# Batch 0's query sketch with tokens as rows, one numerator path, W_out in 2 KB rows, and a new order of work

## The chip, the cores and the metric

The kernel runs on one core of one Trainium2 chip. The metric is the device time of one execution in microseconds; of several executions the median is given. The core has five instruction streams that run side by side and meet only at semaphores: TensorE (PE; its weight loads are shown apart as PEld), VectorE (DVE), ScalarE (ACT), GpSimd (POOL) and SyncE (SP). In this kernel SP only issues DMAs; ScalarE issues a few.

## What is computed

Attention with polynomial sketches in four batches of four heads, 1088 tokens and 32 dimensions, then a feed-forward stage with a tanh shrink over all 4352 tokens:

```python
def phi(x):                      # r = 8, so 64 features
    a = np.einsum('rd,bhsd->bhsr', S1, x)
    b = np.einsum('rd,bhsd->bhsr', S2, x)
    return np.einsum('bhsi,bhsj->bhsij', a, b).reshape(*x.shape[:-1], 64)
q_p, k_p = phi(q), phi(k)
kv  = np.einsum('bhsf,bhsd->bhfd', k_p, v)
z   = np.sum(k_p, axis=2)
num = np.einsum('bhsf,bhfd->bhsd', q_p, kv)
den = np.einsum('bhsf,bhf->bhs', q_p, z)[..., None] + 1e-06
x = (num / den).transpose(0, 2, 1, 3).reshape(4352, 128)
h = x @ w_in                     # 128 -> 2048
out = (h - np.tanh(h)) @ w_out   # 2048 -> 128
```

Inputs and output are fp32. The attention matmuls run in fp32, the feed-forward ones in bf16.

## The kernel before

**A planned order.** The program is a list of operations (`_Prog.add`) with the tiles that they read and write. `TABLE` is the order, written out: each token is an operation's number, the engine that runs it (`v`, `a`, `g`, `t`, `s` for VectorE, ScalarE, GpSimd, TensorE, SP) and the buffers that it takes; `f` and `F` are matmuls on zeros of 256 and 512 columns (L423, L424). `plan` walks through the table, gives out buffers and adds a dependence for each reuse of one; it also holds a big load back until all but 1.45 MB of the big loads ahead of it have landed. `sync` turns dependences into semaphore waits, and `emit` writes the five streams. Each engine runs its own operations strictly in the table's order. An operation can carry `lock=True`; before, nothing reads it.

**Attention of a batch.** k is transposed by VectorE in 32x32 blocks (L530), sketched by TensorE (L575), and transposed back into `abk` (L587). A gram matrix of the two k sketches (L602) is copied out (`gm`), multiplied by S2 (`scmm`, L612 or L614) and copied into the query's weights (`wqd` for batch 0, `wq` through `scx` and `sc`, L622 and L626, for the others): this gives the denominator as one more sketch column group. The 64 products of a token's two k sketches are formed in `w` (L642) by VectorE or GpSimd, and 36 matmuls (L657) multiply them by v. The result is copied four times over (`kvd`), transposed on TensorE (L675) and copied to `kvb`. q is transposed by VectorE (L567) and sketched by TensorE with the sketch weights stationary (L753, 32x32 tiles of the array); the result comes back to tokens as rows by a VectorE transpose into `abc` (L758). Then `m`, `den`, `rd`, `aq` (tile `ap`) form the first sketch divided by the denominator (L770 to L778); `qp` (L796) forms the products, `qpT` (L801) transposes them, `num` (L812) multiplies them by `kvb`, and two copies `x` put the tokens into `xT`, the feed-forward input, in bf16.

**Batch 0** has two parts. Its first 384 tokens take a path of their own, `q_heads` with `kv_heads` (L685 to L731): K·V in a block-diagonal form `kvd_68`, the sketch as one 128x128 matmul (L700), `abc` by a VectorE transpose (L703), and the numerator as four fp32 matmuls (L731). Its other 704 tokens take the common path.

**Weights.** W_in is loaded in four pieces of 512 columns and cast to bf16 (`wi`, L353); W_out likewise (`wo`), its loads in rows of 512 bytes: partition `ji` takes row `jb * 128 + ji`. W_in is also transposed on TensorE (L881, `wit`) and copied (`wiT`), and W_in times W_out is formed once (L895) and split into `wch` and `wcl`.

**Feed-forward.** The tokens go in ten groups (`GCOLS`: 384, 352, 352, six of 512, 192). A group has 16 matmuls `h` (L917) of up to 512 tokens, each into a PSUM bank out of three; ScalarE takes tanh of it (`th`, L921), which frees the bank; 16 matmuls `o` (L938) add up the output, and two matmuls (L942) with `wch` and `wcl` add the linear part. From the eighth group on two banks are taken at a time, and for part of the columns of groups 5 to 8 VectorE adds the linear part (L926). The group's result is transposed by VectorE (`ot`, L947) into one of three tiles and stored by four or eight DMAs (L957).

## Time and profile before

| | us |
|---|---|
| median of 3 runs | 104.42 (103.82 to 105.89) |
| the profiled execution | 105.08 |
| its span, first to last instruction | 102.8 |
| PE busy / DVE / ACT / POOL | 96.5 / 79.5 / 79.1 / 36.4 |
| first feed-forward matmul | 17.16 |
| batch 1's numerator | 40.28 |
| last transpose of the output | 99.43 |
| bytes moved | 11.37 MB |

A busy PE isn't PE at its peak: the end of a matmul is modelled, and zero matmuls count as busy. A row of the timeline gives the start, the busy time, the engine, the line, the operation, the tiles (written <- read), the shapes and the count; in brackets stands how long the engine was idle before it and what ended that. SPq and ACTq are DMA issues. fp32 matmuls appear as two passes, so a group of 36 has a count of 72. Numbers of lines are those of the kernel before.

### The profile page before, as it was taken

Reading aid. Unit: us, or ns where it says so; the run is one execution under the profiler, and the core shown is the slowest. Engines: PE = TensorE matmul, PEld = TensorE weight load, DVE = VectorE, ACT = ScalarE, POOL = GpSimd, SP = SyncE. Lnnn points to the kernel's source line nnn. Section 1 sums busy time; section 2 is a strip of 40 time slices with the busy share of each in tenths; the row PEclk is TensorE's granted clock in tenths of the full one; section 3 lists DMA queues with packets and bytes.
Section 4 is the critical chain, followed back from the end, with each engine's and each line's share of the span. In section 5 each row is a group of like instructions: output and inputs, shape, how many; then the busy total and the mean of one; then the engine's idle time right before and its main releaser. Section 6 shows DMA issues by size and latency. Waiting matters only on the chain.

```text
span 102.8 us, 3036 instructions
## 1 busy us (share of the span) xinstructions
PE 96.5 (94%) x1260; PEld 48.2 (47%) x1260; DVE 79.5 (77%) x145; ACT 79.1 (77%) x157; POOL 36.4 (35%) x54
## 2 busy tenths in 40 slices
PE   5999979999969999999999999999999999999960
PEld 2343556466625545453733444343454444445650
DVE  1669799759748999798579699678899789999530
ACT  4001298986559989799899698999996999999940
POOL 3079845740044594099994890000000000000000
PEclk9999999999999999999999999999999999999999
DMA  2887968979999670311300003304200320501555
GB/s 69 269 270 228 298 216 244 307 223 282 323 267 242 169 183 0 53 24 28 48 0 6 0 0 55 54 0 68 34 0 11 57 41 0 90 12 17 79 74 83
DMA packets 25917, 11.37 MB, mean 111 GB/s; under 512 B 19120, under 2 KB 23600, under 8 KB 25904
## 3 DMA queue, kind: packets, MB, share of 16 engines
q1 hardware_dynamic: 24288, 10.98, 42.2%
q10 hardware_dynamic: 1616, 0.20, 1.3%
q8 instruction: 10, 0.16, 0.7%
q14 instruction: 3, 0.02, 0.1%
HBM read 8.95 MB, written 2.23 MB: 109 GB/s over the span
## 4 chain that ended last, share of the span: by engine, by line
PE 68%; DMA 15%; SPq 10%; DVE 2%; issue 1%
PE psb L917 27%; PE psb L938 27%; SPq L459 10%; DMA wi_f<-in_moe_w_in_dram 6%; DMA wo_f<-in_moe_w_out_dram 5%; PE psb L812 4%; DMA qL<-in_q_dram 4%; PE psb L942 3%; PE psb L753 2%; PE psb L657 2%; DVE qT L567 1%; PE psb L575 1%; DVE abk L587 1%; PE psb L602 0%; PE psb L675 0%
## 5 line engine op out<-in xcount | busy, mean ns | idle before, releaser
L917 PE MATMUL psb<-xT,wi 128*128 128x512 bf16 (+3 forms) x160 | 48.8, 349 | 0.0
L921 ACT ACTIVATE th<-psb 128x512 bf16<-128x512 f32 (+3 forms) x77 | 40.5, 599 | 2.8 <-PE psb L917 2.4
L938 PE MATMUL psb<-th,wo 128*128 128x512 bf16 (+3 forms) x90 | 26.4, 343 | 0.1
L917 PEld LDWEIGHTS psb<-xT,wi 128*128 128x128 bf16 x160 | 14.7, 97 | 23.1 <-ACT th L921 4.1
L921 ACT ACTIVATE wi_f<-psb 128x512 bf16<-128x512 f32 (+3 forms) x31 | 16.6, 623 | 1.6 <-PE psb L917 1.5
L921 ACT ACTIVATE wo_f<-psb 128x512 bf16<-128x512 f32 (+2 forms) x28 | 16.7, 630 | 1.4 <-PE psb L917 1.3
L796 POOL TENSOR_TENSOR qp<-ap,abc 128x768 f32<-128x768 f32 x11 | 16.4, 1511 | 3.6 <-DVE ap L778 3.4
L926 DVE TENSOR_TENSOR th<-psb,th 128x320 bf16<-128x320 f32 (+2 forms) x24 | 13.4, 563 | 1.9 <-ACT th L921 1.0
L642 POOL TENSOR_TENSOR w<-abk 128x768 f32<-128x768 f32 x7 | 11.1, 1594 | 8.4 <-DVE abk L587 8.4
L938 PEld LDWEIGHTS psb<-th,wo 128*128 128x128 bf16 x90 | 8.8, 100 | 5.6 <-POOL wo L353 0.5
L938 PE MATMUL psb<-wo_f,wo 128*128 128x512 bf16 (+1 forms) x32 | 10.9, 363 | 0.0
L801 DVE STREAM_TRANSPOSE qpT<-qp 128x768 f32<-128x768 f32 x11 | 10.4, 956 | 0.5 <-POOL qp L796 0.5
L938 PE MATMUL psb<-wi_f,wo 128*128 128x512 bf16 (+2 forms) x38 | 10.3, 344 | 0.0
L947 DVE STREAM_TRANSPOSE ot<-psb 128x512 f32<-128x512 f32 (+3 forms) x10 | 6.3, 633 | 3.4 <-PE psb L938 3.3
L424 PE MATMUL psb<-zz 128*128 128x512 bf16 x24 | 8.1, 468 | 0.0
L926 DVE TENSOR_TENSOR wi_f<-psb,wi_f 128x192 bf16<-128x192 f32 (+1 forms) x12 | 6.1, 510 | 1.6 <-ACT wi_f L921 0.9
L926 DVE TENSOR_TENSOR wo_f<-psb,wo_f 128x320 bf16<-128x320 f32 (+2 forms) x12 | 6.8, 572 | 0.7 <-ACT wo_f L921 0.3
L530 DVE STREAM_TRANSPOSE kT<-kL 128x576 f32<-128x576 f32 (+3 forms) x10 | 5.8, 606 | 1.6 <-DMA kL<-in_k_dram 1.6
L758 DVE STREAM_TRANSPOSE abc<-psb 128x1152 f32<-128x1152 f32 (+1 forms) x4 | 5.1, 1272 | 1.9 <-PE psb L753 1.8
L812 PE MATMUL psb<-qpT,kvb 32*32 32x288 f32 (+1 forms) x256 | 6.2, 392 | 0.0
L567 DVE STREAM_TRANSPOSE qT<-qL 128x1088 f32<-128x1088 f32 (+2 forms) x5 | 5.2, 1057 | 0.6 <-DMA qL<-in_q_dram 0.6
L657 PE MATMUL psb<-w,vL 128*32 128x64 f32 x288 | 5.2, 221 | 0.0
(89 smaller groups left out, 98.1 us busy)
## 6 DMA issues: line engine op xcount, KB each, us to landing
vL<-in_v_dram SPq DMA_DIRECT2D x16, 144.0 KB, 3.8
kL<-in_k_dram SPq DMA_DIRECT2D x8, 272.0 KB, 3.3
qL<-in_q_dram SPq DMA_DIRECT2D x6, 272.0 KB, 4.2
wi_f<-in_moe_w_in_dram SPq DMA_DIRECT2D x4, 256.0 KB, 5.9
wo_f<-in_moe_w_out_dram SPq DMA_DIRECT2D x4, 256.0 KB, 5.6
out_dram<-ot SPq DMA_DIRECT2D x14, 64.0 KB, 2.0
out_dram<-ot SPq DMA_DIRECT2D x8, 48.0 KB, 3.1
qL<-in_q_dram SPq DMA_DIRECT2D x2, 176.0 KB, 3.4
```

Of the source, the lines that this page charges most:

```text
L424: "F": lambda e, n: e.matmul(bank(3), zz.ap[:, 0:128], zz.ap[:, None, 128:384].to_broadcast([128, 2, 256]), start=True, stop=True)}, zop)
L459: op = P.add({x: occ for x in (eng if isinstance(eng, tuple) else (eng,))}, lambda e, n: e.dma_start(out=o_, in_=i_), w=w, dma=(nbytes, nb ...
L642: P.add({**_v(768), **_gt(768)}, lambda e, n: e.tensor_tensor(out=wv.ap.rearrange("p (x i j) -> p x i j", i=8, j=8), in0=abh(0)[:, :, :, N ...
L657: i = e.matmul(pv[b].ap[h * 32:(h + 1) * 32, 0:64], vL[b][:, h, blk * 32:(blk + 1) * 32], wvs[b, p].ap[:, (bi * 4 + h) * 64:(bi * 4 + h + ...
L796: P.add({**_v(cn * 256), **_gt(cn * 256)}, lambda e, n, qp=qp, c0=c0, cn=cn: e.tensor_tensor(out=qp.ap[:, 0:cn * 256].rearrange("p (x i j) ...
L801: P.add(_v(cn * 256), lambda e, n, qp=qp, o0=o0, cn=cn: e.transpose(qt.ap[:, o0 * 256:(o0 + cn) * 256], qp.ap[:, 0:cn * 256]), r=[qp], w=[ ...
L812: i = e.matmul(psa4[h * 32:(h + 1) * 32, g, 0:nb * 32], kvb.ap[g * 32:(g + 1) * 32, x, h * 32:(h + 1) * 32], qq[g * 32:(g + 1) * 32, 0:nb, ...
L917: P.add(_mm(n_), lambda e, n, jb=jb, hv=hv: e.matmul(hv.ap[:, jb % m * 512:jb % m * 512 + n_], wi[jb // 4].ap[:, (jb % 4) * 128:(jb % 4 + ...
L921: act = P.add(_a(n_ * m), lambda e, n, hv=hv, th=th: e.activation(out=th.ap.rearrange("p (u x) -> p u x", u=m)[:, :, 0:n_], in_=hv.ap.rear ...
L926: P.add(_vp(gc * m), lambda e, n, hv=hv, th=th: e.tensor_tensor(out=th.ap.rearrange("p (u x) -> p u x", u=m)[:, :, 0:gc], in0=hv.ap.rearra ...
L938: fn = lambda e, n, x=x, st=st, sp_=sp_: e.matmul(ov.ap[:, 0:n_], wo[x // 4].ap[:, x % 4, :], ths[x][0].ap[:, ths[x][1] * 512:ths[x][1] * ...
L947: P.add(_vp(n_), lambda e, n: e.transpose(ot.ap[:, 0:n_], ov.ap[:, 0:n_]), r=[ov], w=[ot], name=f"ot{gi}")
```

## The change

- **Batch 0's query sketch.** `q_heads` and `kv_heads` are gone. All of batch 0's q is sketched by nine matmuls (three operations of three, `q_sketch0`) in which q's transpose is the stationary side and the weights `wqd`, now 24 columns a head, are the moving one. The result has tokens as rows, and three plain copies on ScalarE bring it into `abc`, in place of VectorE's transposes. The zero columns of `wqd` and their memset go, as does `sc` of batch 0.
- **One numerator path.** The first 384 tokens of batch 0 take the common path, `q_front` and `q_piece`, with `kvd`, its transpose and `kvb` ahead of it.
- **W_out in 2 KB rows.** Partition `ji` of piece `i` takes the four rows `i * 512 + ji * 4` to `+ 3`, 2 KB in one run. So that W_in's columns agree, its cast reads every fourth column.
- **Turns.** A `lock` operation on VectorE waits for the last `lock` operation before it on GpSimd, and the other way round.
- **Loads.** Three of batch 0's v loads and one of W_in are issued by ScalarE, and v waits until the second half of k has landed.
- **New order.** All of `TABLE` is new. By the engines' streams: the program opens with twelve long zero matmuls; ScalarE's queue is `abc0.0`, `abc0.6`, a W_in cast, `kvd0`, a W_in cast, `abc0.3`, `kvb0`, `wiT0` and the copy of the first tokens; ScalarE also casts a third W_in piece and two W_out pieces, GpSimd the rest; the W_in cast `wi2` stands ahead of the first tanh; W_out's loads stand ahead of batch 1's v and batch 2's k; of the three k products of a batch, batch 0 has two on VectorE (before: one) and batch 1 none (before: all three); VectorE takes the q transposes of batches 1 and 2 ahead of `abc` of batch 1; `gm` of batches 2 and 3 go to VectorE, `kvb` of 2 and 3 to ScalarE; output stores are issued later and in another order.

```diff
--- before.py
+++ after.py
@@ TABLE @@
...
@@ plan @@
+        lastl = {"vector": None, "gpsimd": None}
...
+            if o.lock and e in lastl:
+                d = lastl["gpsimd" if e == "vector" else "vector"]
+                if d is not None:
+                    o.deps.setdefault(d, False)
+                lastl[e] = o
@@ tiles @@
-    qpTh_p = pool("qpTh", 2, [128, 6 * 64])
-    wqd = sb("wqd", [128, H, 32])
+    wqd = sb("wqd", [128, H, 24])
-    kvd0 = sbv("kvd0", [128, 2, 128])
-    P.add(_g(32), lambda e, n: e.memset(wqd[:, :, 24:32], 0.0), w=[wqdc], name="wqdz")
@@ loads @@
-                load_s(1, S2, ("scalar", "sync"))
+                load_s(1, S2, "sync")
...
-            load(vL[b][:, h, :], src, [vvals[b][h]], 128 * 1152, 128, ("sync", "scalar") if b == 0 else "sync", name=f"lv{b}.{h}", occ=640.0)
+            load(vL[b][:, h, :], src, [vvals[b][h]], 128 * 1152, 128, ("sync", "scalar") if b == 0 else "sync", name=f"lv{b}.{h}", occ=640.0, wait=[x for x in P.ops if x.name == "lk0.1"] if b == 0 else ())
...
-    wos = moe_w_out.rearrange("(jb ji) c -> ji jb c", jb=NJB, ji=128)
+    wos = moe_w_out.rearrange("(i ji jb) c -> ji i (jb c)", i=4, jb=4)
...
-        load(wof[i].ap, wos[:, i * 4:(i + 1) * 4, :], [wof[i]], 128 * 2048, 512, name=f"lwo{i}")
+        load(wof[i].ap.rearrange("p j c -> p (j c)"), wos[:, i, :], [wof[i]], 128 * 2048, 128, name=f"lwo{i}")
@@ batch 0's q @@
-    def kv_heads():
...
-    def q_heads(i):
...
+    def q_sketch0(s0, s1, abc):
+        outs = []
+        for j, a in enumerate(range(s0, s1, 3)):
+            pq = _Val(first1)
+
+            def sk(e, n, a=a, pq=pq):
+                for k in range(3):
+                    i = e.matmul(pq.ap[:, k * 96:(k + 1) * 96], qTs[0][:, (a + k) * 128:(a + k + 1) * 128], wqd.rearrange("p h f -> p (h f)"),
+                                 start=True, stop=True, skip_group_check=True)
+                return i
+            P.add(_pe(550, 230.0), sk, r=q_in(0, a, a + 3) + [wqds, wqdc], w=[pq], mode="128x128", name=f"qsk0.{a}")
+            outs.append((j, a, pq))
+        for j, a, pq in outs:
+            P.add({**_a(288), **_vp(288)}, lambda e, n, a=a, pq=pq: copy(
+                e, n, abc.ap[:, a - s0:a - s0 + 3, :, 0:24], pq.ap[:, 0:288].rearrange("p (k h f) -> p k h f", h=H, f=24)),
+                r=[pq], w=[abc], name=f"abc0.{a}")
...
-            cn = 2 if left in (2, 4) else min(left, 3)
+            cn = 2 if left in (2, 4) or (b, s0) == (0, 0) else min(left, 3)
+            cn = min(cn, left)
...
-        q_sketch(b, s0, s1, abc)
+        q_sketch0(s0, s1, abc) if b == 0 else q_sketch(b, s0, s1, abc)
...
-        kv_heads()
-        q_heads(0)
+        kv_tail(0)
+        q_transpose(0, 0)
+        st = q_front(0, 0, 3)
+        q_piece(0, 0, 0, 3, *st)
@@ weights @@
-            P.add({**_as(512), **_g(512), **_v(512)}, lambda e, n, i=i: copy(e, n, wi[i].ap[:, :], wif[i].ap), r=[wif[i]], w=[wi[i]], name=f"wi{i}", lock=True)
+            P.add({**_as(512), **_g(512), **_v(512)}, lambda e, n, i=i: copy(
+                e, n, wi[i].ap.rearrange("p (b j) -> p b j", b=4), wif[i].ap.rearrange("p (j b) -> p b j", b=4)), r=[wif[i]], w=[wi[i]], name=f"wi{i}", lock=True)
```

More of the change, by code (lines that the diff above doesn't have):

```diff
@@ L70 @@
+821v:1 823s 824a 825a 822s
 """
@@ L544, in s_weights @@
         for i, (w, z) in enumerate(zip(wqc, wqs)):
+            if i == 0:
+                continue
             P.add(_g(8), lambda e, n, z=z: e.memset(z[:, 24:32], 0.0), w=[w], name=f"wqz{i}")
@@ L631, in gram @@
                 e, n, wqds.ap, pg.ap[:, 64:96].rearrange("p (h i) -> p h i", h=H)), r=[pg], w=[wqds], name="wqs0")
-            P.add(_v(32), lambda e, n: e.tensor_reduce(
-                out=wqs[b][:, 16:24], in_=wqds.ap.rearrange("p h i -> p i h"), op=ALU.add, axis=AX.X),
-                r=[wqds], w=[scv[b]], name=f"sc{b}")
     wvs = {}
@@ L680, in kv_tail @@
             r=[pv[b]], w=[kvb], name=f"kvb{b}")
-    kvh = _Val(ap=sb("kvh", [128, 64]))
-    def kv_heads():
-        P.add(_vp(64), lambda e, n: e.transpose(kvh.ap, pv[0].ap[:, 0:64]), r=[pv[0]], w=[kvh], name="kvh")
-        P.add({**_v(256), **_gt(256)}, lambda e, n: e.tensor_tensor(
-            out=kvd0.ap.rearrange("p x (h v) -> p x h v", h=H),
-            in0=kvh.ap.rearrange("p (x v) -> p x v", x=2)[:, :, None, :].to_broadcast([128, 2, H, 32]),
-            in1=maskh.ap[:, None, :, None].to_broadcast([128, 2, H, 32]), op=ALU.mult),
-            r=[kvh, maskh], w=[kvd0], name="kve", lock=True)
@@ L853, in attention @@
         q_transpose(0, 1)
-        kv_tail(0)
         st = q_front(0, 3, 9)
```

128 lines of the change are left out of this document (42 added, 86 removed).

## The prediction

> **What bounds the kernel now.** I read the page's busy times, then busy time by stretch, then the chain that ended last. Stretches show PE, PEld, DVE, ACT and POOL busy with counts, the granted clock, the DMA share and GB/s.
>
> ```profile
> PE 96.5 (94%) x1260; PEld 48.2 (47%) x1260; DVE 79.5 (77%) x145; ACT 79.1 (77%) x157; POOL 36.4 (35%) x54
> ...
> 0.00:17.16 17.16, 15.17 (x222) 7.70 (x223) 12.56 (x31) 6.45 (x12) 9.61 (x28) 1.00 0.74 226
> 17.16:40.28 23.12, 22.20 (x384) 11.73 (x390) 18.43 (x30) 18.67 (x51) 11.04 (x12) 1.00 0.81 232
> 40.28:99.43 59.15, 59.11 (x667) 28.82 (x666) 48.13 (x85) 53.99 (x95) 15.73 (x14) 1.00 0.20 31
> ```
> ```profile
> 7.15 5.79 DMA wi_f<-in_moe_w_in_dram
> ...
> 23.04 4.41 DMA qL<-in_q_dram
> 27.47 1.31 DVE qT L567
> 28.78 0.74 DVE abk L587 x2
> 29.66 1.04 PE psb L753 x32
> ...
> 40.28 1.53 PE psb L812 x63
> ...
> 51.04 0.22 PE psb L675 x2
> ...
> 99.43 0.38 DVE ot L947
> ```
>
> There are three stretches. Until 17.16 batch 0's attention runs, and much of TensorE's work is the zero matmuls of L424. From 17.16 to 40.28 FFN and attention of batches 1 and 2 share TensorE; the chain goes through loads until batch 1's q (27.47), its sketch (29.66) and its numerator (40.28). After 40.28 TensorE is full for 59.1 of 59.15 us. ScalarE idles 4.45 us in the second stretch and 5.2 in the third. So three things can move the end: the start of the FFN, batch 1's numerator, and ScalarE, once it has less slack than it is given work. The last transpose starts at 99.43 of a 102.8 span; that tail keeps its four stores on SP and ACT.
>
> **The start, step by step.** These rows carry it.
>
> ```profile
> 1.31 4.08 PE L424 MATMUL psb<-zz 128*128 128x512 bf16 x10
> 6.42 0.81 PE L424 MATMUL psb<-zz 128*128 128x512 bf16 x3
> 6.50 2.02 SPq L459 DMA_DIRECT2D wi_f<-in_moe_w_in_dram  x4
> 7.31 0.34 PE L602 MATMUL psb<-abk 128*32 128x32 f32 x17
> 7.33 1.51 POOL L642 TENSOR_TENSOR w<-abk 128x768 f32<-128x768 f32 x1 [0.49 <-DVE abk L587]
> 8.38 0.18 ACT L353 COPY wqd<-psb 128x32 f32<-128x32 f32 x1 [0.43 <-PE psb L614]
> 8.43 1.23 DVE L642 TENSOR_TENSOR w<-abk 128x768 f32<-128x768 f32 x1
> 9.03 0.30 PEld L700 LDWEIGHTS psb<-qT,wqd 128*128 128x128 f32 x2 [0.46 <-POOL wqd L442]
> 10.41 1.23 PE L657 MATMUL psb<-w,vL 128*32 128x64 f32 x72
> 11.57 1.04 PE L424 MATMUL psb<-zz 128*128 128x512 bf16 x4
> 12.31 0.62 ACT L353 CAST wi<-wi_f 128x512 bf16<-128x512 f32 x1 [3.75 <-DMA wi_f<-in_moe_w_in_dram]
> 12.84 0.36 ACT L353 COPY kvd<-psb 128x256 f32<-128x256 f32 x1
> 13.25 0.44 PE L675 MATMUL psb<-ident,kvd 128*128 128x128 f32 x2 [0.64 <-ACT kvd L353]
> 15.13 1.52 PE L731 MATMUL psb<-qpTh,kvd 128*128 128x192 f32 x8
> 16.56 0.55 ACT L353 CAST xT<-psb 128x192 bf16<-128x192 f32 x2
> 17.16 0.66 PE L917 MATMUL psb<-xT,wi 128*128 128x384 bf16 x3
> ...
> 23.60 1.35 PE L812 MATMUL psb<-qpT,kvb 32*32 32x192 f32 x64
> ```
>
> Zero matmuls: twelve long ones open the program instead of ten and a short one (4.08/10 = 0.41 each), and five and a half instead of three and a half (0.81/3 = 0.27 each) stand ahead of the gram. I let the gram start at 7.8, not 7.31.
>
> Query sketch: before, TensorE waited 0.46 for POOL's memset of `wqd`; that goes. From the gram to the end of the `wqd` copy is 8.56 - 7.31 = 1.25, so the sketch starts at 9.1, as now. Now it ends at 10.41, 1.4 later. The new one is nine fp32 matmuls, each recorded as two passes, of 96 columns with q's transpose as weights. A pass costs 0.22/2 = 0.11 in the transpose of `kvd` (128 columns) and 1.52/8 = 0.19 at L731 (192 columns). So 18 passes cost 2.0 to 3.4. I take 2.0, because 96 columns is nearest the first row; with its zero matmuls it ends at 11.2.
>
> K·V: 1.23 as now, to 12.4. Then `kvd`. Now it stands in ScalarE's queue behind a w_in cast that waits for its load until 12.31, though K·V was done at 11.64. In the new order w_in's first load is the eighth issue on SP (three v loads go to ScalarE's queue), about 4.6 by the present issues; with the 5.8 us it takes now it lands near 10.4, and the cast is over when K·V ends. So `kvd` runs 12.45 to 12.8. If that cover fails, `kvd` is late by as much as the load is. Behind the v loads, which wait for K, stand only the table load and the gram's copy at about 8.
>
> TensorE meanwhile has four zero matmuls (1.04) and one set of W_in transposes (0.25 estimated from 0.22 to 0.44 for two wider ones), so the `kvd` transpose runs 13.7 to 14.1 and `kvb`, now on ScalarE, 14.1 to 14.5. The numerator has 64 passes of 96 columns: under the 1.35 of the 192-column one and, at worst, no cheaper than it. I take 1.1, ending at 15.6, result at 15.85. The copies out run side by side on VectorE and ScalarE (0.55/2 each), so the FFN starts near 16.3, **0.9 earlier**.
>
> VectorE's path to that numerator: two k products behind POOL's turn (7.6 + 1.51 = 9.1, then 0.9 each from the row of three below), four small steps of about 0.25, two products and two transposes of 0.6: 13.5. It has 1 us of cover. The turn by semaphore itself costs no work here: VectorE's product already took 1.23 instead of 0.9 when it began while POOL's ran (8.43 against 8.84).
>
> The bounds of the start are -1.5 (zero matmuls hidden, numerator at 1.0) and +0.6 (sketch at 3.4, less cover).
>
> The Trainium skill speaks against one edit. Its page "SBUF — State Buffer", section "Door 1: The DMA port swizzle", says that SBUF works in 16-byte lines and that each access in a new line pays a penalty. W_out in 2 KB rows makes the W_in casts read every fourth fp32, one per line. No row here shows such a read.
>
> I keep the casts at 0.62, the row of the same size. The nearest row of a read with gaps is POOL's `m` below, eight of every 32 fp32: 0.79/288 = 2.7 ns an element, against 1.51/768 = 2.0 in a product, 1.4 times. The upper end is twice 0.62, an estimate: each element a second access. Three of the four casts are on ScalarE: one ahead of `kvb` (+0.6 at that end) and one ahead of the first tanh (+0.6).
>
> **The middle.**
>
> ```profile
> 8.93 2.10 POOL L642 TENSOR_TENSOR w<-abk 128x768 f32<-128x768 f32 x1
> ...
> 22.14 2.69 DVE L642 TENSOR_TENSOR w<-abk 128x768 f32<-128x768 f32 x3
> ...
> 24.99 0.42 ACT L353 CAST xT<-psb 128x320 bf16<-128x320 f32 x1 [0.79 <-PE psb L812]
> ...
> 28.23 0.37 ACT L353 COPY kvb<-psb 128x256 f32<-128x256 f32 x1
> ...
> 30.80 1.38 DVE L758 STREAM_TRANSPOSE abc<-psb 128x1152 f32<-128x1152 f32 x1 [1.29 <-PE psb L753]
> ...
> 32.26 0.79 POOL L770 TENSOR_TENSOR m<-abc 128x288 f32<-128x288 f32 x1 [1.16 <-DVE abc L758]
> ...
> 33.13 0.21 ACT L353 COPY gm<-psb 128x32 f32<-128x32 f32 x1
> ...
> 34.56 4.45 POOL L796 TENSOR_TENSOR qp<-ap,abc 128x768 f32<-128x768 f32 x3 [1.51 <-DVE ap L778]
> ```
>
> The first copied tokens (batch 0's second part) follow the start. In the new order its numerator stands behind `scx`, and `scx` behind POOL's first k product of batch 1; queued behind `scx` on VectorE are batch 2's k transposes. From 14.0 POOL has five short steps of about 0.6 (a W cast's time) and three products of 1.51: 21.5. TensorE comes to the numerator 23.60 - 17.16 = 6.4 after the start, as now: 22.7. So the turn has 1 us of cover; without it batch 2's transposes and this numerator are late by the rest of a product, up to 1.5.
>
> Batch 1: equal bytes precede its q on the queues in both orders. W_out's four loads are ahead of it, in 2 KB instead of 512 B pieces, and SP no longer stops for W_in so late. If the rate is unchanged (226, then 232 GB/s), q arrives as now. The DMA engines idle 0.26 of 17.16 us and 0.19 of the next ten, 6.4 us; if a fifth of it goes, q is 1.3 earlier. VectorE takes both batches' q transposes (1.31 each) ahead of `abc`, and batch 2's q comes 0.56 MB later, 2.4 us. So `abc` ends near 31.0 instead of 32.18, or, with the rate unchanged, as now. From there to the numerator it is 40.28 - 32.18 = 8.1 now: 2.4 until POOL's first product, 4.45 for three, the rest for transposes. In the new order it is 2.4, a product on VectorE (0.9), `scx` (0.2), two on POOL (3.0), a transpose (0.9) and up to 0.7 for an output transpose in between: 8.1 again.
>
> ScalarE gets ahead of that numerator two W_out casts (0.62, as W_in's), a copy of 0.5 (0.42 at five sixths of its size) and loses the gram copy (0.21) and two tanh (0.4 each), +0.7, and one W_in cast (0.62) before its first tanh. With the present idle of 4.45 the start's gain would be gone; without the wait for batch 1's q it is at 38.9. I take the numerator at 39.1, **1.2 earlier, start included**; bounds -2.2 and +0.2.
>
> **The rest.** TensorE's work is the same to 0.2. ScalarE takes two `kvb` (0.37 each), a larger x copy and one tanh or two from before, less a gram copy: +1.3 into 5.2 us of idle. Nothing to all of it may come back; I take +0.5, nearer to nothing, because TensorE is the full one (59.11 of 59.15). Output stores stand in a new order on SP; a transpose that reuses a tile waits for its old stores. They are issued a group or more ahead in the order, which hides them; without that cover one transpose is late by a landing:
>
> ```profile
> out_dram<-ot SPq DMA_DIRECT2D x14, 64.0 KB, 2.0
> ```
>
> **Sum.** -1.2 + 0.5 = -0.7. The profiled execution took 105.08, 2.28 beyond its span and 0.66 above the median, so it would be 104.4; against the median of 104.42 the forecast is **103.7**. From no change a measurement of this kernel can tell about 2%.
>
> **Rivals.** *The start carries through.* The start is at its lower bound (-1.5), the 0.92 that TensorE is seen idle in the second stretch (23.12 - 22.20) goes with the earlier q, and ScalarE's additions vanish in its idle time: -2.4, 102.0. The load at 27.47 speaks for it, the equal 8.1 us behind it against it.
>
> *ScalarE becomes the bound.* It has 18.67 + 53.99 = 72.7 busy us behind the start and gets 2.7 more (three casts 1.86, copies 1.24, less 0.42), one cast of it ahead of the first tanh. If its idle comes from dependences and stays, the first tanh is 0.75 earlier and the last 2.1 - 0.75 = 1.4 later: 105.8. With the strided casts at twice their time, 1.2 more: 107.0, slower. It decides from +2.1, that is, once a strided cast takes 0.97 and the idle stays. The 5.2 us of idle in the full stretch speak against it; that each FFN matmul needs a bank that a tanh frees speaks for it.
>
> *The change doesn't do what it says:* the turns take nothing away, since the two engines already exclude each other at 8.43, and W_out's rows matter only if the load rate bounds. Then only the new order counts, at 104.4.
>
> **How the numbers follow.** Forecast 0.50, of it the case of 104.4 0.15; the start carries through 0.18; ScalarE the bound 0.32, 0.24 of it with the casts' price and beyond 106.5. Range 101.7 to 107.0, which takes in both rivals' times and leaves less than 2 in 10 outside; the likeliest case alone spans 102.5 to 104.9. Faster by over 2% (under 102.3) 0.18, within 2% 0.58, slower (over 106.5) 0.24.
>
> **What would show it.** First FFN matmul near 16.3; the sketch's passes near 0.11; W_in casts at 0.62, or near 1.2 if the lines count; the numerator of batch 1 at 39.1; ScalarE's idle after it under 4 us; no wait over 0.5 between VectorE and POOL that TensorE then waits for. Wrong if the W_in loads land after 12, if a turn holds VectorE ahead of a transpose that TensorE needs, or if tanh comes late in the third stretch.

## The result and the profile after

The changed kernel is slower by 0.7%: 105.24 us median (104.08 to 107.57, 20 runs) against 104.44 (103.48 to 105.89, 20 runs) of the kernel before, ratio 1.0066 with a 95% interval of 1.0040 to 1.0093. The forecast was 103.7. The loss is smaller than the 2% by which one measurement can tell a change, but its interval lies clear of 1. All ratios here take only each kernel's undisturbed runs within 1.5% of its fastest, so they can differ from the quotient of two medians, most where a kernel's times spread widely.

The busy times of the page after, and busy time by the same three stretches (until the first FFN matmul, until batch 1's numerator, until the last output transpose; columns as in the prediction):

```profile
PE 96.5 (93%) x1305; PEld 50.0 (48%) x1305; DVE 77.9 (75%) x140; ACT 82.0 (79%) x161; POOL 35.9 (35%) x50
```
```profile
0.00:16.89 16.89, 15.43 (x264) 8.96 (x265) 10.77 (x26) 7.02 (x13) 7.10 (x28) 1.00 0.75 234
16.89:40.55 23.66, 21.82 (x389) 12.03 (x394) 18.17 (x30) 19.83 (x52) 15.40 (x14) 1.00 0.69 211
40.55:99.81 59.26, 59.22 (x667) 28.97 (x667) 48.55 (x86) 55.15 (x98) 13.42 (x10) 1.00 0.22 35
```

TensorE's work is the same to the tenth (96.5 each). The stretches took 16.89, 23.66 and 59.26 us where they took 17.16, 23.12 and 59.15: the start gained 0.27, the middle lost 0.54, the full stretch lost 0.11. Behind the last transpose's start stand 3.59 us (103.4 - 99.81) instead of 3.37. Together that is +0.60, the difference of the spans (103.4 to 102.8). TensorE idled 1.84 us in the middle stretch (23.66 - 21.82), twice the 0.92 of before. So the start gained too little, and something new stands in the middle.

The chain that ended last, after (start, length, what), names both; its first three rows are the new sketch:

```profile
9.50 0.68 PE psb L691 x6
10.28 0.64 PE psb L691 x6
11.04 0.66 PE psb L691 x6
12.12 1.06 ACT wi L359
13.45 1.03 ACT wi L359
...
16.50 1.04 ACT wi L359
...
25.73 0.91 PE psb L659 x54
26.64 1.58 issue
28.22 0.49 PE psb L659 x18
...
40.55 1.53 PE psb L775 x63
```

Before, no cast of W_in was on this chain. Now three are, of over 1 us each. And inside batch 1's K·V (L659) stands 1.58 us of "issue", time in which TensorE waits for nothing that the profile shows. In the order of time, the start of the same trace:

```profile
12.01 1.17 ACT L359 CAST wi<-wi_f 128x512 bf16<-128x512 f32 x1
13.08 0.37 ACT L359 COPY kvd<-psb 128x256 f32<-128x256 f32 x1
13.34 1.14 ACT L359 CAST wi<-wi_f 128x512 bf16<-128x512 f32 x1
...
14.67 0.38 ACT L359 COPY kvb<-psb 128x256 f32<-128x256 f32 x1
...
16.40 1.14 ACT L359 CAST wi<-wi_f 128x512 bf16<-128x512 f32 x1
17.42 0.51 ACT L886 ACTIVATE th<-psb 128x384 bf16<-128x384 f32 x1
```
```profile
7.96 0.34 PE L607 MATMUL psb<-abk 128*32 128x32 f32 x17
...
9.34 0.84 PE L691 MATMUL psb<-wqd,qT 128*128 128x96 f32 x6
...
11.72 1.21 PE L659 MATMUL psb<-w,vL 128*32 128x64 f32 x72
...
15.20 0.95 PE L775 MATMUL psb<-qpT,kvb 32*32 32x96 f32 x64 [0.16 <-ACT kvb L359]
...
16.89 0.49 PE L882 MATMUL psb<-xT,wi 128*128 128x384 bf16 x2
```

A W_in cast takes 1.14 to 1.17 us instead of 0.62. One stands ahead of `kvd`, one ahead of `kvb`, one ahead of the first tanh. The middle, from a timeline of all engines:

```profile
25.66 0.98 PE L659 MATMUL psb<-w,vL 128*32 128x64 f32 x54
...
26.70 1.29 DVE L572 STREAM_TRANSPOSE qT<-qL 128x1088 f32<-128x1088 f32 x1
...
28.22 0.49 PE L659 MATMUL psb<-w,vL 128*32 128x64 f32 x18 [1.58 <-issue]
...
28.75 0.37 ACT L359 COPY kvd<-psb 128x256 f32<-128x256 f32 x1 [2.37 <-PE psb L659]
...
29.05 1.31 DVE L572 STREAM_TRANSPOSE qT<-qL 128x1088 f32<-128x1088 f32 x1 [1.05 <-DMA qL<-in_q_dram]
...
31.23 1.38 DVE L720 STREAM_TRANSPOSE abc<-psb 128x1152 f32<-128x1152 f32 x1 [0.87 <-PE psb L715]
```

Each fp32 matmul is recorded as two passes, so x54 of 72 means that K·V stopped behind matmul 27 of 36. ScalarE waited 2.37 us for its end. The transpose at 26.70 is of batch 1's q, the one at 29.05 of batch 2's. `abc` of batch 1 began at 31.23, where it began at 30.80 before.

### The profile page after: what moved, and what is told of

It is laid out like the page before. It is cut to its first block, busy times and chain, and to the rows that moved or that the text cites. A ratio compares the mean times of both kernels' runs of the same rounds, so it can differ in the third digit from the quotient of the medians.

```text
span 103.4 us, 3128 instructions
## 1 busy us (share of the span) xinstructions
PE 96.5 (93%) x1305; PEld 50.0 (48%) x1305; DVE 77.9 (75%) x140; ACT 82.0 (79%) x161; POOL 35.9 (35%) x50
## 4 chain that ended last, share of the span: by engine, by line
PE 89%; ACT 5%; issue 2%; DVE 1%
PE psb L882 30%; PE psb L903 29%; PE psb L775 7%; PE psb L428 7%; PE psb L659 4%; PE psb L580 3%; ACT wi L359 3%; PE psb L907 3%; PE psb L715 2%; PE psb L691 2%; PE psb L607 1%; PE psb L860 1%; ACT abc L359 1%; PE psb L677 1%; PE psb L617 0%
## 5 line engine op out<-in xcount | busy, mean ns | idle before, releaser
L886 ACT ACTIVATE th<-psb 128x512 bf16<-128x512 f32 (+3 forms) x135 | 70.5, 611 | 3.5 <-PE psb L882 2.7
L903 PE MATMUL psb<-th,wo 128*128 128x512 bf16 (+3 forms) x159 | 42.8, 347 | 0.0
L891 DVE TENSOR_TENSOR th<-psb,th 128x192 bf16<-128x192 f32 (+2 forms) x48 | 26.0, 553 | 4.7 <-ACT th L886 2.3
L903 PEld LDWEIGHTS psb<-th,wo 128*128 128x128 bf16 x159 | 15.1, 98 | 10.4 <-DVE den L735 0.5
L759 POOL TENSOR_TENSOR qp<-ap,abc 128x768 f32<-128x768 f32 (+1 forms) x10 | 14.1, 1424 | 11.0 <-DVE qp L759 6.2
L644 POOL TENSOR_TENSOR w<-abk 128x768 f32<-128x768 f32 x9 | 13.6, 1517 | 2.7 <-DVE abk L592 1.9
L764 DVE STREAM_TRANSPOSE qpT<-qp 128x768 f32<-128x768 f32 (+2 forms) x13 | 11.4, 893 | 0.1
L775 PE MATMUL psb<-qpT,kvb 32*32 32x288 f32 (+2 forms) x320 | 7.0, 364 | 0.2 <-ACT kvb L359 0.2
L659 PE MATMUL psb<-w,vL 128*32 128x64 f32 x288 | 5.3, 221 | 1.6 <-issue 1.6
L659 PEld LDWEIGHTS psb<-w,vL 128*32 128x32 f32 x288 | 4.3, 110 | 3.3 <-issue 2.8
L720 DVE STREAM_TRANSPOSE abc<-psb 128x1152 f32<-128x1152 f32 x3 | 4.1, 1383 | 1.2 <-PE psb L715 1.2
L775 PEld LDWEIGHTS psb<-qpT,kvb 32*32 32x32 f32 x320 | 3.9, 103 | 2.2 <-issue 1.0
```

The source lines that it names most:

```text
L644: P.add({**_v(768), **_gt(768)}, lambda e, n: e.tensor_tensor(out=wv.ap.rearrange("p (x i j) -> p x i j", i=8, j=8), in0=abh(0)[:, :, :, N ...
L659: i = e.matmul(pv[b].ap[h * 32:(h + 1) * 32, 0:64], vL[b][:, h, blk * 32:(blk + 1) * 32], wvs[b, p].ap[:, (bi * 4 + h) * 64:(bi * 4 + h + ...
L759: P.add({**_v(cn * 256), **_gt(cn * 256)}, lambda e, n, qp=qp, c0=c0, cn=cn: e.tensor_tensor(out=qp.ap[:, 0:cn * 256].rearrange("p (x i j) ...
L764: P.add(_v(cn * 256), lambda e, n, qp=qp, o0=o0, cn=cn: e.transpose(qt.ap[:, o0 * 256:(o0 + cn) * 256], qp.ap[:, 0:cn * 256]), r=[qp], w=[ ...
L775: i = e.matmul(psa4[h * 32:(h + 1) * 32, g, 0:nb * 32], kvb.ap[g * 32:(g + 1) * 32, x, h * 32:(h + 1) * 32], qq[g * 32:(g + 1) * 32, 0:nb, ...
L886: act = P.add(_a(n_ * m), lambda e, n, hv=hv, th=th: e.activation(out=th.ap.rearrange("p (u x) -> p u x", u=m)[:, :, 0:n_], in_=hv.ap.rear ...
```

## The experiments

Three theories were to be told apart. A: the strided W_in casts cost the time. B: the stop inside K·V costs it, and TensorE stops there for want of instructions. C: the turns between VectorE and GpSimd cost or save it. Every run had five rounds beside the kernel before on the same chip. A ratio's interval is 0.3% to 0.5% to either side, so two ratios of different kernels are told apart from about 0.5% to 0.7% on.

| kernel | median us | kernel before beside it, median us | ratio to before | 95% interval |
|---|---|---|---|---|
| the changed kernel | 105.24 | 104.44 | 1.0066 | 1.0040 to 1.0093 |
| plain casts, rows kept | 104.77 | 104.15 | 0.9973 | 0.9931 to 1.0016 |
| plain casts, 512 B rows | 104.75 | 104.15 | 0.9961 | 0.9915 to 1.0008 |
| no turns | 105.90 | 104.15 | 1.0166 | 1.0131 to 1.0201 |
| before with 2 KB rows and strided casts | 105.42 | 104.15 | 1.0098 | 1.0062 to 1.0133 |
| before with turns | 104.72 | 104.06 | 1.0045 | 1.0009 to 1.0082 |
| zero matmuls split | 103.88 | 104.06 | 0.9955 | 0.9922 to 0.9988 |
| 512 B rows, no turns | 105.07 | 104.06 | 1.0002 | 0.9952 to 1.0051 |
| 512 B rows, three FFN steps first | 104.76 | 104.06 | 0.9996 | 0.9949 to 1.0043 |
| 512 B rows, split | 103.75 | 104.28 | 0.9931 | 0.9900 to 0.9962 |
| split, no turns | 103.83 | 104.28 | 0.9954 | 0.9916 to 0.9991 |
| eight zero matmuls split | 104.62 | 104.28 | 1.0026 | 0.9989 to 1.0063 |
| before, split | 105.43 | 104.28 | 1.0069 | 1.0034 to 1.0105 |
| 512 B rows, split, no turns | 103.54 | 104.34 | 0.9918 | 0.9886 to 0.9951 |
| 512 B rows, split, FFN first | 103.95 | 104.34 | 0.9988 | 0.9963 to 1.0014 |
| plain casts, rows kept, split | 103.32 | 104.34 | 0.9917 | 0.9875 to 0.9959 |

### The casts

The changed kernel with W_in cast in plain order:

```diff
-                e, n, wi[i].ap.rearrange("p (b j) -> p b j", b=4), wif[i].ap.rearrange("p (j b) -> p b j", b=4)), r=[wif[i]], ...
+                e, n, wi[i].ap[:, :], wif[i].ap), r=[wif[i]], ...
```

> The changed kernel with the W_in cast reading its columns in order, while W_out stays in 2 KB rows; left out is the reordering of W_in's columns, so the feed-forward stage pairs wrong columns with wrong rows. Theory A (the strided casts, 1.10 to 1.17 instead of 0.62, are what ate the start): casts at 0.62, first tanh at 16.4 to 16.7 instead of 17.42, whole kernel 0.7 to 1.1 below the changed kernel, that is 104.1 to 104.5. Rival B (TensorE's 1.6 us stop inside batch 1's K.V product, with no wait in the program there, is the loss, and whatever comes earlier ahead of it is lost in it): the casts get short, but the product's end stays within 0.3 of 28.7 and the time stays within 0.3 of 105.2.

The same with W_out in 512 B rows again, so that the computation is whole:

```diff
-    wos = moe_w_out.rearrange("(i ji jb) c -> ji i (jb c)", i=4, jb=4)
+    wos = moe_w_out.rearrange("(jb ji) c -> ji jb c", jb=NJB, ji=128)
-        load(wof[i].ap.rearrange("p j c -> p (j c)"), wos[:, i, :], [wof[i]], 128 * 2048, 128, name=f"lwo{i}")
+        load(wof[i].ap, wos[:, i * 4:(i + 1) * 4, :], [wof[i]], 128 * 2048, 512, name=f"lwo{i}")
```

> The changed kernel with W_out back in 512 B rows and W_in cast in order. Compared with the run before it, only W_out's rows differ. If the rows matter through the load rate, q of batch 1 and 2 land 0.5 to 1.0 later than there and the time is 0.3 to 0.8 higher. If not, both times agree within 0.3. Theory A: 104.1 to 104.5, rival B: 105.2.

And the other way round: rows and strided casts put into the kernel before.

```diff
-    wos = moe_w_out.rearrange("(jb ji) c -> ji jb c", jb=NJB, ji=128)
+    wos = moe_w_out.rearrange("(i ji jb) c -> ji i (jb c)", i=4, jb=4)
...
-... copy(e, n, wi[i].ap[:, :], wif[i].ap) ...
+... copy(e, n, wi[i].ap.rearrange("p (b j) -> p b j", b=4), wif[i].ap.rearrange("p (j b) -> p b j", b=4)) ...
```

> The kernel before with W_out in 2 KB rows and the strided W_in casts that go with it, nothing else. Theory A: four casts of 1.14 on ScalarE ahead of the first copies out, first feed-forward matmul 1.0 to 2.0 later than 17.16, time 0.8 to 1.8 above the kernel before. If the 2 KB rows bring loads earlier by what the casts cost: within 0.3 of the kernel before.

The groups of casts by shape (busy, mean ns), first of the changed kernel, then of the run with plain casts, then of the kernel before with strided ones:

```profile
L359 ACT CAST wi<-wi_f 128x512 bf16<-128x512 f32 x3 | 3.4, 1147 | 0.0
L359 POOL CAST wi<-wi_f 128x512 bf16<-128x512 f32 x1 | 1.1, 1101 | 0.0
```
```profile
L359 ACT CAST wi<-wi_f 128x512 bf16<-128x512 f32 x3 | 1.9, 622 | 0.0
```
```profile
L353 ACT CAST wi<-wi_f 128x512 bf16<-128x512 f32 x4 | 4.3, 1112 | 3.3 <-DMA wi_f<-in_moe_w_in_dram 3.3
```

A strided cast takes 1147/622 = 1.84 times a plain one. In the kernel before, rows and strided casts cost 1.0% (its one profiled execution, 107.42 us, is read for the casts' length alone). In the changed kernel plain casts are worth 0.9% by the ratios (1.0066 to 0.9973) and, with 512 B rows, 1.0% (to 0.9961). But the times of these two runs spread widely, and by the medians of all their runs (104.77 and 104.75 against 104.15) they gain only 0.2% on the changed kernel (105.24 against 104.44). So theory A holds in its direction, its size in this kernel is open, and the rows by themselves bring nothing that can be measured. The timeline of the run with 512 B rows shows the earlier start, and the stop still there:

```profile
11.23 1.21 PE L659 MATMUL psb<-w,vL 128*32 128x64 f32 x72
...
16.04 0.49 PE L882 MATMUL psb<-xT,wi 128*128 128x384 bf16 x2
16.40 1.79 ACT L886 ACTIVATE th<-psb 128x384 bf16<-128x384 f32 x4
...
26.95 0.49 PE L659 MATMUL psb<-w,vL 128*32 128x64 f32 x18 [0.93 <-issue]
```

The first tanh is 1.0 earlier than the 17.42 of the changed kernel. Half of that is not the casts': batch 0's K·V, which waits for no cast, ended at 12.44 here (11.23 + 1.21) and at 12.93 there. From that end to the first FFN matmul the changed kernel took 3.96 and this one 3.60, to the first tanh 4.49 and 3.96, so the casts cost about 0.4 and 0.5 us there. The stop stood behind matmul 27 once more, now 0.93 long, and K·V ended at 27.4 instead of 28.7; in this execution it did not swallow the gain. With the rows kept, the one profiled execution (106.38 us) stood there for 2.27 and ended K·V at 28.3, near the rival's 28.7. So the rival is not excluded by these two runs; the next section takes the stop away.

### The stop

The page after counts the fetches of instructions in a DMA queue of their own (packets, MB, share):

```profile
q8 instruction: 10, 0.16, 0.6%
```

Ten fetches of 0.16 MB are 16 KB each. Counting every instruction that the trace records on TensorE (matmuls, weight loads, a few semaphore events), the stop in K·V came behind the 961st in the changed kernel, in both runs with plain casts and in the first run without turns, which began at 25.3 to 27.3 us. In the changed kernel the fetch ahead of it began at 25.84 and took 0.88; TensorE went on at 28.22. So theory B says that the place belongs to the count of instructions. It was tested by adding instructions without adding work: each 512-wide zero matmul as two of 256.

```diff
-               "F": lambda e, n: e.matmul(bank(3), zz.ap[:, 0:128], zz.ap[:, None, 128:384].to_broadcast([128, 2, 256]),
-                                          start=True, stop=True)}, zop)
+               "F": lambda e, n: [e.matmul(bank(3)[:, h * 256:(h + 1) * 256], zz.ap[:, 0:128], zz.ap[:, 128:384],
+                                           start=True, stop=True) for h in range(2)][1]}, zop)
```

> The changed kernel with each 512-wide zero matmul issued as two of 256, so TensorE has the same work at the start in 46 more instructions (23 matmuls with their weight loads). Theory A (the stop inside batch 1's K.V is TensorE waiting for its next block of 256 instructions): the stop stays but moves about 46 instructions earlier in the program, that is 46/4 = 11 to 12 of the four-instruction fp32 matmuls: from behind matmul 27 of the 36 to behind 15 or 16. It lasts 1 to 2.5 us and the time stays within 0.5 us. Rival B (it waits for a load or a semaphore of that place): it stays behind matmul 27.

```profile
25.56 1.21 PE L659 MATMUL psb<-w,vL 128*32 128x64 f32 x72
...
38.81 1.60 PE L775 MATMUL psb<-qpT,kvb 32*32 32x288 f32 x64
```

The timeline of this run shows K·V in one piece and batch 1's numerator at 38.81 instead of 40.47 by the same view; the time fell by 1.1% (1.0066 to 0.9955). The expectation that the stop would move to another place was not met: it went. The fetch came earlier (23.13, by the trace), and the 256 instructions that end with the 961st now held more FFN work and took 4.0 us instead of 3.3, so the next block was there in time. A smaller shift, eight of the opening zero matmuls split, had to show the place:

```diff
-... 54g 50v F F F F F F F F F F F F 64t:0 62g
+... 54g 50v f f f f f f f f f f f f f f f f F F F F 64t:0 62g
```

> The changed kernel with only eight of the twelve zero matmuls that open it split in two: 16 instructions more, the same work. Theory (blocks of 256 instructions): where TensorE stops inside batch 1's K.V, it stops four fp32 matmuls earlier, behind matmul 23 of the 36 instead of 27 (in the trace behind 46 recorded passes instead of 54), and the time stays within 0.7 us of the changed kernel. Rival (a load or a semaphore at that place): behind 27 again.

```profile
25.16 0.87 PE L659 MATMUL psb<-w,vL 128*32 128x64 f32 x46
26.77 0.61 PE L659 MATMUL psb<-w,vL 128*32 128x64 f32 x26 [0.73 <-issue]
```

It did, to the matmul: behind 46 passes, matmul 23, four earlier for 16 instructions more. No load and no semaphore moved there. The stop is TensorE at the end of the instructions that had been fetched.

The same split in the kernel before:

> The kernel before with its 512-wide zero matmuls split in two. Theory (the split helps only where a block boundary falls into a run of fp32 matmuls; before shows stops of 1.02 us at 12.2 and 28.5, which other waits of those places may cover): between 0.7 us faster and 0.5 us slower than before. If splitting helped in itself, by a warmer start, it would be 1 us faster as in the changed kernel.

```profile
14.22 0.49 PE L881 MATMUL psb<-identb,wi 128*128 128x128 bf16 x6 [0.79 <-issue]
...
27.34 0.46 PE L575 MATMUL psb<-kT,wab 64*32 64x288 f32 x1 [0.33 <-issue]
```

Here it cost 0.7%, a little more than the 0.5 us that was expected at most. Splitting does not help in itself. Behind the 449th and the 961st instruction this kernel now has two stops marked "issue"; before, the idle times near these places (0.64 and 0.82) ended with `kvd` and `abk`. That the new stops are the 0.7% is not shown: the one profiled execution, 104.34 us, was the fastest of its twelve (median 105.43) and its span is shorter than that of the kernel before (102.2 for 102.8).

Three FFN steps moved ahead of batch 1's K·V were to cover the fetch:

```diff
-131g:2 132t:0 133t 134t 128v 138v 319t:0 354t:1 281t 270t:2 ...
+131g:2 319t:0 354t:1 281t 132t:0 133t 134t 128v 138v 270t:2 ...
```

> The 512 B run with three FFN steps (two input tiles and one output tile, about 0.33 us each) moved from behind batch 1's K.V to ahead of it. Theory A (the stop waits for a fetch of instructions that starts at a place in the program and takes 0.9 us plus some 1.4 until TensorE goes on): three FFN steps now lie within that time, the stop of 0.93 to 1.14 in K.V shrinks by up to 1.0, and the total falls by up to 0.5 us. Rival B (the stop is bound to the arrival at K.V or to the fetch's start, which moves as well): the stop stays at about 1 us, K.V ends 1 us later and the total is the same or up to 1 us more.

> 512 B rows, plain casts, split zero matmuls, and three FFN steps moved ahead of batch 1's K.V. Theory (the split alone had already taken the stop away, so the move only delays K.V by three steps of 0.33 that other work fills): within 0.3% of the kernel without the move (0.69% under before). Rival (the first run with the move had the earliest numerator of all, 38.34, because the move covers the fetch better): 0.3% or more below it, over 1% under before.

In the profile of the first of these, K·V ran from 25.34 to 26.55 without a stop and the numerator began at 38.34, the earliest of the runs with 512 B rows. Its ratio was 0.9996 all the same, with times from 103.13 to 108.04: the one profiled execution was its best. With the zero matmuls split as well it was 0.9988, against 0.9931 without the move. Neither expectation was met. Where there is no stop, the move gains nothing (it costs 0.6% by these ratios, 0.1% by the medians), and it is no cure.

### The turns

The changed kernel without the turns:

```diff
-            if o.lock and e in lastl:
-                d = lastl["gpsimd" if e == "vector" else "vector"]
-                if d is not None:
-                    o.deps.setdefault(d, False)
-                lastl[e] = o
```

> The changed kernel without the turns of VectorE and GpSimd. Prediction's view (the engines exclude each other in any case): within 0.3 of 105.2, two-input products stretched where they overlap. Rival C (the turns hold VectorE ahead of work that TensorE needs): 0.5 or more below 105.2, with the numerator of batch 0's second part earlier than 23.1.

It was slower by 1.0% (1.0066 to 1.0166), which neither theory had. Two things differ in its profile. The products of the first 16 us, by shape, in the changed kernel and without turns (line numbers are 5 lower there):

```profile
L644 DVE TENSOR_TENSOR w<-abk 128x768 f32<-128x768 f32 x2 | 1.8, 955 | 0.4 <-POOL w L644 0.4
...
L759 POOL TENSOR_TENSOR qp<-ap,abc 128x256 f32<-128x256 f32 x1 | 0.6, 629 | 3.7 <-DVE qp L759 3.7
```
```profile
L639 DVE TENSOR_TENSOR w<-abk 128x768 f32<-128x768 f32 x2 | 2.1, 1089 | 0.0
...
L754 POOL TENSOR_TENSOR qp<-ap,abc 128x256 f32<-128x256 f32 x1 | 1.1, 1132 | 2.8 <-DVE ap L735 2.8
```

Without turns the products overlap and are longer, 1.13 against 0.63 and 1.09 against 0.96. But VectorE no longer waits 0.4 for its turn, and the two about cancel. The other is a new stop, in batch 0's numerator, behind 27 passes, the 449th instruction:

```profile
15.55 0.44 PE L770 MATMUL psb<-qpT,kvb 32*32 32x96 f32 x27 [0.15 <-ACT kvb L354]
16.33 0.73 PE L770 MATMUL psb<-qpT,kvb 32*32 32x96 f32 x37 [0.34 <-issue]
```

The first fetch began at 13.6 there and at 11.25 in the changed kernel. To tell the two apart, the turns were taken out of the run with 512 B rows, and out of the two with split zero matmuls (the same lines in each), and put into the kernel before (the same lines added).

> The changed kernel with 512 B rows and plain casts (the run of that name), and the turns taken out as well. If the turns are worth what the first run without them said (1.0 us on the changed kernel), this is 1.0 us slower than the 512 B run, about 105.5 to 106.0, with GpSimd's and VectorE's products stretched where they overlap. Rival (the first run without turns lost its time because TensorE's first fetch of instructions came at 13.6 instead of 11.25 and stopped the numerator at 15.75, which need not come again): within 0.4 us of the 512 B run, with the stretched products but no stop in batch 0's numerator.

> The changed kernel with split zero matmuls, and the turns taken out. With the turns (the run of split zero matmuls) it was 0.45% under the kernel before, with no stop in batch 1's K.V. Theory A (turns keep GpSimd's and VectorE's products of the start from stretching one another, worth 0.4 us ahead of the numerator): 0.4 to 1.0 us slower than with turns, the first FFN matmul at 17.1 or later. Rival B (the 1 us that taking them out cost was again a stop of TensorE): within 0.3 us of the run with turns.

> 512 B rows, plain casts, split zero matmuls, and no turns. Theory (turns are worth nothing by themselves): within 0.3% of the same kernel with turns, which was 0.69% under the kernel before. Rival (turns are worth something once casts no longer hold the start): 0.4% or more slower than that.

> The kernel before with the turns alone: each product or copy that takes the turn on VectorE waits for the last one on GpSimd, and the other way round; order, loads and casts as before. Theory A (turns keep the products of the two engines from stretching one another, as the run without turns suggested: 768-wide product on VectorE 2.10 instead of 1.83 for two, GpSimd's 256-wide one 1.13 instead of 0.63): the VectorE products that overlap GpSimd's at 8.43 take their undisturbed 0.9, and the time falls by 0.3 to 1.0 us. Rival B (the prediction's: turns take nothing away, since the two engines exclude each other anyway): within 0.3 us of the kernel before. Rival C (the order before was not made for turns, so one holds VectorE back ahead of a transpose that TensorE needs): 0.5 to 2 us slower, with a wait of VectorE for GpSimd of 1 us or more in the second stretch.

Where the blocks' ends lie elsewhere, taking the turns out changes nothing: 0.9954 against 0.9955, and 0.9918 against 0.9931. With 512 B rows alone it costs 0.4% (0.9961 to 1.0002, which the intervals do not tell from nothing), and its profile has the stop in the numerator again, longer:

```profile
16.20 0.73 PE L770 MATMUL psb<-qpT,kvb 32*32 32x96 f32 x37 [0.85 <-issue]
```

So the turns are worth nothing by themselves, and the loss without them goes with the stop. That the stop is all of the 1.0% is not shown: it lasts 0.34 us, and in that profile the sketch began 0.36 later than in the changed kernel (9.70 for 9.34), the numerator ended 0.91 later, and the span is 0.6 longer (104.0 for 103.4). In the kernel before the turns cost 0.45%, as the third expectation there had it, but not through VectorE in the second stretch. GpSimd's second product, which K·V needs, ran from 8.93 for 2.10, to 11.03; with the turns it waits for VectorE's:

```profile
9.33 0.96 DVE L648 TENSOR_TENSOR w<-abk 128x768 f32<-128x768 f32 x1 [0.37 <-POOL w L648]
```
```profile
10.37 1.51 POOL L648 TENSOR_TENSOR w<-abk 128x768 f32<-128x768 f32 x1 [0.95 <-DVE w L648]
```

It ends at 11.88, 0.85 later. Of that, 0.49 had come before the wait (without it the product would have begun at 9.42, 0.49 behind the 8.93 of before), so the turn itself cost 0.36 in this profile. Each product is at its own shortest, and the last is late. The new order gives that second product to VectorE.

### Both costs taken away

> The 512 B run (plain casts) with the zero matmuls split as well. Theory (the two costs of the changed kernel are its strided casts, 1.0 us, and the stop of TensorE at the end of a block of 256 instructions, about 1.1 us, and they stand in different stretches): they add, so this is about 2 us under the changed kernel and about 1.2 us (1.2%) under the kernel before; first FFN matmul near 16.0 and batch 1's numerator near 38. Rival (the earlier start brings the stop back, since the fetch then comes in the thick of the loads): no better than the run with split zero matmuls alone, with a stop of 1 us or more in or about batch 1's K.V.

> The changed kernel with 2 KB rows kept, W_in cast in plain order (which leaves out the reordering of columns that the rows need) and the zero matmuls split. Theory (strided casts and stop are separate costs that add): about 2 us under the changed kernel, 1.2% to 1.4% under before, first FFN matmul near 16.1. Rival (one hides behind the other, as the split run with 512 B rows suggests): 0.5% to 0.8% under before.

These are the edits of the cast and of the zero matmuls together, with 512 B and with 2 KB rows. They are 0.7% and 0.8% under the kernel before, short of the 1.2% or more that both theories said, and with the run without turns (0.8%) the three fastest here. The second, in the timeline:

```profile
16.33 0.48 PE L882 MATMUL psb<-xT,wi 128*128 128x384 bf16 x2
...
25.55 1.21 PE L659 MATMUL psb<-w,vL 128*32 128x64 f32 x72 [0.56 <-ACT th L886]
...
39.09 1.33 PE L775 MATMUL psb<-qpT,kvb 32*32 32x288 f32 x47
```

Against the changed kernel that is -1.5% (1.0066 to 0.9917), where plain casts alone gave -0.9% and the split alone -1.1%. With the stop gone, plain casts are worth 0.25% to 0.4% by the ratios, which the intervals do not tell from nothing. So the two costs seem not to add in full. The profiles show one reason: with plain casts TensorE waits for a tanh ahead of batch 1's K·V (0.56 above, 0.44 with 512 B rows), and K·V begins at 25.55 and 25.65, no earlier than with strided casts (25.56). The kernel that computes the whole and beats both is the one with 512 B rows, plain casts and split zero matmuls, with turns (0.9931) or without (0.9918).

## Why the prediction was wrong, point by point

It forecast -0.7 us and the measurement gives +0.7. Two steps failed. The larger is on the path to batch 1's numerator: nothing was put between batch 1's K·V and its `kvd`, and TensorE stood there for 1.58 us. The smaller is a term: a strided W_in cast was put at 0.62 and takes 1.14. With the stop alone gone the ratio is 0.9955; with both gone it is 0.9931 (512 B rows) and 0.9917 (2 KB rows), and the forecast was 103.7/104.42 = 0.993. In the last of these the first FFN matmul is at 16.33 (forecast 16.3) and batch 1's numerator at 39.09 (39.1). That the start agrees so closely is luck: there batch 0's K·V ended 0.39 late (12.79 for 12.4), and the way from it to the FFN took 3.54 us for 3.9.

- **"I keep the casts at 0.62."** Wrong. They take 1.14 to 1.17 on ScalarE, 1.10 on GpSimd. The upper end, twice 0.62, was near. The two places named for it, ahead of `kvb` and ahead of the first tanh, are where casts stand on the chain; a third stands ahead of `kvd`. From the end of batch 0's K·V to the first FFN matmul the changed kernel took 3.96, the run with plain casts and 512 B rows 3.60, so at the FFN's start the casts cost 0.4. The page "SBUF — State Buffer" of the Trainium skill, section "Door 1: The DMA port swizzle", which was weighed there, says that an access in a new 16-byte line pays a penalty. The runs agree: 1.84 times for a read of every fourth fp32. The 1.4 times from `m` was the nearest row, and a read of eight neighbours out of 32 is not the same thing.
- **"From there to the numerator ... 8.1 again"**, and batch 1 1.2 earlier. The step that failed is the one ahead of it: nothing was forecast between K·V and `kvd` of batch 1. There TensorE stopped for 1.58 us, `abc` began at 31.23 and ended at 32.6 instead of 31.0. With no stop the numerator came at 38.8 with the strided casts kept and at 39.1 with plain ones. The rest of this path was right. Batch 1's q landed 1.7 earlier than before (25.76 for 27.45 by the trace; forecast 1.3), `abc` ended at 30.4 to 31.5 in the seven profiles of the new order that have no stop, and from there to the numerator it was 7.9 in the changed kernel. The rows of before showed 10 fetches in their queue, and I did not read them as something that TensorE could wait for.
- The sketch: 0.11 a pass was forecast; six passes took 0.64 to 0.68 on the chain. Right. It started at 9.34 by the timeline, not 9.1, and ended at 11.7, not 11.2, behind a gram at 7.96 instead of 7.8. So K·V ended at 12.93 for a forecast of 12.4, which is 0.53 of the 0.59 by which the FFN's start missed its forecast (16.89 for 16.3); from K·V to the FFN 3.96 stood against 3.9, since that allowance was wide enough to hide the casts. In the profiles of the new order the sketch began anywhere from 8.74 to 9.79, and no run shows why.
- The numerator of batch 0's first part: 0.95, where 1.1 was forecast and 1.0 named as the bound. It began at 15.20 for a forecast of 14.5; in both runs with plain casts it began at 14.5, behind a K·V that had ended half a microsecond earlier.
- **Turns cost nothing.** Right as a total (0.9954 against 0.9955), and so is its reason, that a product was already longer beside the other engine's. "The two engines already exclude each other", as a rival has it, was wrong: before, VectorE's and GpSimd's products both ran, and both longer (1.23 and 2.10 for 0.96 and 1.51 with turns), so in these rows a turn takes away about as much as it adds. The page "SBUF — State Buffer" of the Trainium skill, section "Who interferes with whom", says that a VectorE instruction with two SBUF inputs contends with a GpSimd one that reads SBUF. The rows agree.
- **2 KB rows.** That they matter only if the load rate bounds was said in a rival, and they changed nothing that the intervals tell: 0.9961 with 512 B and 0.9973 with 2 KB rows.
- **The rest, +0.5.** The full stretch took 59.26 for 59.15, +0.11. ScalarE's busy time in it rose from 53.99 to 55.15 and went into its idle time (5.16 to 4.11). The tail behind the last transpose's start, which had no term, took 0.22 more (3.59 for 3.37). The nearer end of the range held.
- **The rivals.** "ScalarE becomes the bound" had the right sign and the right price for a cast, but the wrong mechanism: in the changed kernel ScalarE stood on the chain at the start only. "The start carries through" needed what the stop took. "The change doesn't do what it says" is right of its parts: rows and turns bring nothing, the rest of the change is worth 0.7% to 0.8% once the casts are plain and the stop is gone.

The range of 101.7 to 107.0 held the time. The span given to the likeliest case alone, 102.5 to 104.9, is not the sum of its bounds: -2.2 to +0.2 and 0 to +1.3 on 104.42 give 102.2 to 105.9. Of what the profile would show, the sketch's passes and the W_in casts, near 1.2 if the lines count, came as named, and ScalarE's idle time just missed (4.11 for "under 4"); the stop was in none of it.

## What to carry to other kernels

Price a strided operand by a row with the same stride, or take the dear end: a cast is cheap to leave on a path until its read skips elements. When a new order puts long runs of fp32 or other many-instruction matmuls close together, count TensorE's instructions: a stop marked "issue" in the middle of such a run, at the same count in every run, was here a block of instructions that came late, and a few dozen instructions more ahead of it moved it or took it away. An experiment that changes the number of instructions or the time of a fetch can win 1% by this alone, as splitting the zero matmuls did, so a small loss or gain should be read in the trace before it is believed. And the same step lies up to 1 us apart in the profiles here (the sketch at 8.74 to 9.79): measure a step from the end of the one ahead of it, not from the start of the span.

## What the runs showed of the hardware

TensorE's instructions come in 16 KB blocks through a DMA queue of their own (ten fetches, 0.16 MB, for 2634 recorded instructions). Stops of this kind stood behind the 449th and the 961st recorded instruction only, 512 apart, in seven profiles of this study, and one moved by four fp32 matmuls for 16 instructions. In those seven TensorE went on 1.4 to 1.6 us after the fetch's packets had ended (in the changed kernel 28.22, after 25.84 + 0.88). In the changed kernel the fetch began 2.70 after TensorE had begun the 705th instruction, 256 ahead of the 961st, and those 256, most of them of fp32 matmuls, were used up in 3.28; 2.70 + 0.88 + 1.50 is 5.08, so TensorE stood. With the zero matmuls split, 1.17 + 0.88 + 1.50 = 3.55 stood against 4.02, and no stop is seen. Over all seventeen profiles, TensorE stopped behind the 961st in the six in which these 256 were used up in 3.1 to 3.3 us, and in none of the eleven in which that took 4.0 to 5.6. The page "Runtime: NRT & Kernel Launch" of the Trainium skill, section "Instruction fetch mechanics", gives blocks of 16 KiB or 256 instructions, refilled through the sequencer's own queue, and calls the cost of crossing one mostly hidden. The size agrees; hidden it was not in these places, with 0.3 to 2.3 us a stop. Why a fetch begins sooner in one kernel than in another (the first one 0.2 to 1.9 us after the 193rd instruction in the runs with the new order and turns, 2.9 to 3.5 in three of the four without turns) stays open: no run here changed the load on the queues alone.

A read of every fourth fp32 costs ScalarE 1.84 times a plain one (1147 ns for 622) and GpSimd 1.8 times (1101 for 611). Two-input products on VectorE and GpSimd that overlap are longer than the same ones apart, up to 1.13 for 0.63.
